# Gate weights of a routed mixture in an fp32 attention and expert kernel: earlier load, products held until landing, one block's logits on one engine

## The chip, the cores and the metric
One Trainium2 chip, one core. The metric is device time in microseconds (us) of one execution. Three runs of the kernel before took 834.63 us in the median (833.44 to 834.67).

## What is computed
Three layers run one after the other, in fp32.

```python
for t in range(S):      # batch 4, 8 heads, S = 768, head_dim 48
    cur = einsum('bhd,bhe->bhde', u * k[t], v[t])
    y[t] = einsum('bhd,bhde->bhe', r[t], state + cur)
    state = w[t][..., None] * state + einsum('bhd,bhe->bhde', k[t], v[t])
h = x @ w_in            # 3072 x 384 -> 2048
x2 = (h * sigmoid(1.702 * h)) @ w_out
logits = x2 @ w_gate    # 8 experts, 384 tokens each
# greedy over all (token, expert) pairs by falling logit, capacity 384
out[mask_e] = relu(x2[mask_e] @ w1[e]) @ w2[e]
```

The order of the logits decides which token goes to which expert, so they are computed to fp32 precision.

## The kernel before
The program is recorded by a planner in Python (class Issue, line 66). Every piece of work is a generator that emits instructions and then yields the engines and times that it expects them to need. The planner keeps a clock and a busy time for each engine and resumes the generators by rank, so its cost figures and its estimates of a load's landing decide the order in which instructions stand on each engine. They do not decide when an instruction runs: on the chip each engine takes its instructions in order and waits on semaphores.

The attention is cut into 24 units of 128 time steps of one batch (unit, line 975), three to a block of 384 tokens. A unit runs decay scans on VectorE (L996, L1001), products of keys and queries with the decays (L1013, L1017, L1020), score matmuls (L1032, L1068), a transpose (L1085), output and state matmuls (L1145, L1150, L1100), and writes its rows of the next layer's input as two halves (L1178 high part, L1181 the subtraction for the low part).

The dense layer (class Ffn, line 1193) runs over 8 blocks and, in each, over 16 slices f of the 2048 columns: nine matmuls of 128x384 into a PSUM buffer g (L1204; high and low parts give three products for each of three row groups), gelu and split (L1250, L1253 on ScalarE, L1256 on VectorE, which frees g), then nine matmuls into three accumulators (L1232), two slices behind. There are two g buffers, so slice f + 2 needs the one of slice f free. Half of block 0 comes first, then block 1, then the rest of block 0, then blocks 2 to 7. The weights come as 16 chunks, each split into high and low parts on VectorE and ScalarE (L773 to L828); for the first nine TensorE corrects each half of a chunk (L806 to L808).

The routing needs logits. For blocks 0 to 6 they are taken from the stored rows of x2 and the gate weights, spread over all 128 partitions (wgB, two tiles, loaded in gate_weights, line 1409): dots (line 1283) multiplies a row tile by two experts' weights at a time on VectorE (L1290) and lets ScalarE sum each of the two (L1279). For block 7 the logits come from TensorE straight from the gelu output (L1464), with w_out times w_gate, formed beforehand in wog and wogp: wog_steps (line 1353) loads the small gate weights wg8, transposes them (L1361), computes four slices on TensorE (L1372, L1384) and the other twelve with dots. The planner puts spin, small bf16 matmuls whose result is not used (L729), into PE's order where its clock has PE waiting.

The places around the change are ORDER (line 691), which sets by hand the first loads on SyncE's (SP) queue; the load and the fixed yield in wog_steps; and the two lines that say when the spread weights count as present:

```python
nc.scalar.dma_start(wg8, dram(w_gate, 0, [[Dm, E], [1, Dm]]))   # L1357
yield 3.0
```

Of the kernel before, what the change touches and what calls it, by code (L numbers as in the profile page):

```python
# [8 lines left out]
F32 = mybir.dt.float32  # L9
# [7 lines left out]
OP = mybir.AluOpType  # L17
# [10 lines left out]
CW = 256  # L28
# [14 lines left out]
def dram(ap, off, dims):  # L43
    return bass.AP(tensor=ap.tensor, offset=ap.offset + off, ap=dims)
# [461 lines left out]
def kernel(ctx, tc, r, k, v, w, rk, u, us, w_in, w_out, w_gate, w1, w2, out):  # L506
    nc = tc.nc
    V, A, P, T = nc.vector, nc.scalar, nc.gpsimd, nc.tensor
    H, D = u.shape
    B, NC = r.shape[:2]  # L510
    Dm = H * D
# [3 lines left out]
    E, NC3 = w1.shape[:2]  # L515
# [3 lines left out]
    KT = Dm // 128  # L519
    cap = NT // E  # L520
    NBLK = NT // NB
# [6 lines left out]
    NCVA, NCVB, NCVC = 3, 2, 3  # L528
# [29 lines left out]
    consts = ctx.enter_context(tc.tile_pool(name="consts", bufs=1))  # L558
    wpool = ctx.enter_context(tc.tile_pool(name="wpool", bufs=32))
    ff = ctx.enter_context(tc.tile_pool(name="ff", bufs=2))  # L560
    cv = ctx.enter_context(tc.tile_pool(name="cv", bufs=1))
# [8 lines left out]
    sc = Issue()  # L570
# [117 lines left out]
    tiny = consts.tile([1, 1], F32, name="tiny")  # L688
    V.memset(tiny, 0.0)
    A.activation(tiny, tiny, AF.Gelu_apprx_sigmoid)  # L690
    ORDER = "0wkr us 1wkr 0v 2wkr W0 1v 2v W1 W2 W3 3wkrv"
    BACK = 6
    back = []
    for x in ORDER.split():
        if x == "us":
            nc.sync.dma_start(usel, us)
        elif x[0] == "W":
            load_w(int(x[1]))
        else:
            load(int(x[0]), x[1:])  # L700
# [571 lines left out]
    router = Router(nc, sc, consts, bank, NJ, E, cap)  # L1272
    WGD = E * Dm // 2
    wgB = []

    def sums(t_, i, put):
        yield from sc.room("A", 0.2)
        for n in range(2):
            A.activation(t_[:, n], t_[:, n], AF.Copy, accum_out=put[n])  # L1279
        yield (("A", 0.85),)  # L1280
        R["cvb"].free(i)

    def dots(x, put, slack, rank):

        for e in range(0, E, 2):
            while not R["cvb"].ok() or sc.busy["V"] > sc.t + slack:
                yield 0.02
            i = R["cvb"].new()
            t_ = cv.tile([128, KT * CW], F32, name="cvb", bufs=NCVB).rearrange("p (a d) -> p a d", a=2)
            V.tensor_tensor(t_, x[:, None, :].to_broadcast([128, 2, Dm]),  # L1290
                            wgB[e // 4][:, (e % 4) * Dm:(e % 4 + 2) * Dm].rearrange("p (a d) -> p a d", a=2), op=OP.mult)
            yield (("V", 0.88),)
            sc.add(sums(t_, i, [put(e + n) for n in range(2)]), rank)

    def logits(j, x2, ring, free_x2):
        while not wgB:
            yield 0.5
        yield from dots(x2, lambda e: router.L[:, j, e:e + 1], 0.5, 2.8)
        free_x2(ring)
        todo[0] -= 1  # L1300

# [22 lines left out]
    def store_x2(blk, tt, acc):  # L1324
        c, b = units[blk * NU + tt]
        j = b * NC + c
        if blk == 0:
            sc.until(lambda: tt in rest)
            x2, ring = rest[tt]
            V.tensor_tensor(x2, acc, x2, op=OP.add)  # L1330
            sc.busy["V"] += 0.55
        else:
            ring = R["cva"].new()
            x2 = cv.tile([128, Dm], F32, name="cva", bufs=NCVA)
            A.activation(x2, acc, AF.Copy)  # L1335
            sc.busy["A"] += 0.49
        stored.add((blk, tt))
        nc.scalar.dma_start(x2d[j * 128:(j + 1) * 128, :], x2)
        if blk < NBLK - 1:
            todo[0] += 1  # L1340
            sc.add(logits(j, x2, ring, R["cva" if blk else "cvc"].free), 4)
        else:
            R["cva"].free(ring)

# [2 lines left out]
    wog = consts.tile([128, NFS, E], F32, name="wog")  # L1347
    wogp = consts.tile([128, NFS * 2 * E + 128], F32R, name="wogp")

    wg8 = consts.tile([E, Dm], F32, name="wg8")  # L1350
    wgT = consts.tile([128, KT, E], F32, name="wgT")

    def wog_steps():

        while ("out", 0) not in wdone:
            yield 0.5
        nc.scalar.dma_start(wg8, dram(w_gate, 0, [[Dm, E], [1, Dm]]))  # L1357
        yield 3.0
        ps, done = yield from bank()
        for kt in range(KT):  # L1360
            T.transpose(ps[:, kt * E:(kt + 1) * E], wg8[:, kt * 128:(kt + 1) * 128], ident[:E, :E])  # L1361
        A.activation(wgT, ps[:, :KT * E].rearrange("p (k e) -> p k e", k=KT), AF.Copy)
        done()
        yield (("T", 0.2), ("A", 0.2))
        for f in range(FPE):
            while ("out", f // 2) not in wdone:
                yield 0.5
            yield from wait("wT")
            ps, done = yield from spare_bank()
            for kt in range(KT):  # L1370
                for n in range(2):
                    T.matmul(ps[:, kt * 128:(kt + 1) * 128], rhs2(f, n)[:, kt * 128:(kt + 1) * 128], identr[0],  # L1372
                             start=(n == 0), stop=(n == 1))
            yield (("T", 0.68),)
            yield from sc.room("A", 0.4)
            i = R["wT"].new()
            wT = s1p.tile([128, KT * 128], F32, name="wT")
            A.activation(wT, ps[:, :KT * 128], AF.Copy)
            done()
            yield (("A", 0.5),)  # L1380
            yield WTLAG
            ps, done = yield from spare_bank()
            for kt in range(KT):
                T.matmul(ps[:, :E], wT[:, kt * 128:(kt + 1) * 128], wgT[:, kt], start=(kt == 0),  # L1384
                         stop=(kt == KT - 1))
            R["wT"].free(i)
            A.activation(wog[:, f], ps[:, :E], AF.Copy)
            done()
            yield (("T", 0.4), ("A", 0.2))
        while len(wgB) < 2:  # L1390
            yield 0.5
        for f in range(FPE, NFS):
            while not R["wT"].ok() or sc.busy["V"] > sc.t + 0.6:
                yield 0.02
            i = R["wT"].new()
            ws = s1p.tile([128, KT * 128], F32, name="wT")
            V.tensor_tensor(ws, rhs2(f, 0).bitcast(F32), rhs2(f, 1).bitcast(F32), op=OP.add)
            yield (("V", 0.48),)
            yield from dots(ws, lambda e: wog[:, f, e:e + 1], 0.6, 2.9)
            R["wT"].free(i)  # L1400
        while R["cvb"].live:
            yield 0.1
        hi, lo = (wogp[:, :NFS * 2 * E].rearrange("p (f x e) -> p f x e", f=NFS, x=2)[:, :, x]
                  for x in range(2))
        A.activation(hi, wog, AF.Copy)
        V.tensor_tensor(lo, wog, hi.bitcast(F32), op=OP.subtract)
        todo[1] = 1

    def gate_weights():
        while ("out", NCH - 1) not in wdone:  # L1410
            yield 1.0
        for i in range(2):
            t_ = cv.tile([128, WGD], F32, name="raw64", bufs=2)
            nc.scalar.dma_start(t_, dram(w_gate, i * WGD, [[0, 128], [1, WGD]]))
            wgB.append(t_)


# [96 lines left out]
    for s in range(len(seq) + 2):  # L1514
# [5 lines left out]
        if s < len(seq):  # L1520
            blk, f = seq[s]
# [264 lines left out]
    for s in range(E * NF3 + 2):  # L1786
        at[0] = s
        i, f = divmod(s, NF3)
# [71 lines left out]
```

## Time and profile before

| | |
|---|---|
| median of 3 runs | 834.63 us (833.44 to 834.67) |
| the profiled execution | 833.22 us, span 831.5 us |
| TensorE matmul busy | 808.4 us, 97% of the span |
| VectorE, ScalarE, GpSimd busy | 622.4, 484.3, 136.3 us |
| granted TensorE clock, mean | 0.991 of full |

The span runs from the first to the last instruction; the execution's time has the start and end around it. PE is TensorE's matmul side, PEld its weight loads, DVE VectorE, ACT ScalarE, POOL GpSimd, SP SyncE; a q behind a name is that engine's queue of DMA issues and semaphores. The first 140 us hold the weights' splitting and the first units, 150 to 500 us the dense layer with the units beside it, 498 to 536 the last block's first products, and the rest the routing and the experts. An instruction's line is that of the kernel's source; for a helper the same line stands for every use.

### The profile page before, as it was taken

What the parts mean: (1) busy time and instruction counts of PE and PEld (TensorE: products, weight loads), DVE (VectorE), ACT (ScalarE), POOL (GpSimd) and SP (SyncE); (2) the same over time, 40 slices, a digit from 0 to 9 for tenths busy, and PEclk for the clock granted to TensorE, in tenths of its full rate; (3) what the DMA queues carried; (4) which work ended last, traced back from release to release, by engine and by line L of the source; (5) the groups of instructions that cost most, each with busy time, mean ns of one, the idle gap of its engine ahead of it and who ended that gap; (6) DMA issues with size and microseconds to landing.
All of it is one profiled execution on the core that took longest, in us unless ns stands there. A gap on an engine that the chain in (4) does not pass through costs nothing.

```text
span 831.5 us, 17525 instructions
## 1 busy us (share of the span) xinstructions
PE 808.4 (97%) x6593; PEld 759.4 (91%) x6593; DVE 622.4 (75%) x1388; ACT 484.3 (58%) x1226; POOL 136.3 (16%) x188
## 2 busy tenths in 40 slices
PE   8999998999999999999999998999999999999996
PEld 7788998899999999999999998988988988999995
DVE  9957797869879969889878827378888987885310
ACT  5653753476676776786597638405466645675421
POOL 1001000000000100000100100003334354454211
PEclk9999998999999999999999999999999999999998
DMA  9823532332322323213302100008989799989400
GB/s 296 234 90 115 173 138 88 90 102 82 94 58 84 93 57 95 82 57 105 105 24 83 36 3 30 1 23 217 209 236 284 218 232 270 280 223 339 89 29 28
DMA packets 46068, 105.85 MB, mean 127 GB/s; under 512 B 7352, under 2 KB 13344, under 8 KB 45984
## 3 DMA queue, kind: packets, MB, share of 16 engines
q1 hardware_dynamic: 30800, 68.20, 25.7%
q0 software_dynamic: 10416, 29.50, 16.3%
q10 hardware_dynamic: 4768, 7.04, 2.3%
q8 instruction: 51, 0.84, 0.4%
q14 instruction: 33, 0.27, 0.1%
HBM read 73.60 MB, written 10.03 MB: 101 GB/s over the span
## 4 chain that ended last, share of the span: by engine, by line
PE 83%; issue 6%; DMA 4%; ACT 3%; DVE 3%; POOL 1%; ACTq 0%; POOLq 0%; DVEq 0%
PE g L1204 31%; PE acc L1232 31%; PE s L1068 3%; PE s L1150 3%; PE s L429 2%; DMA cvb<-x2d,idx 2%; PE s L1145 1%; PE acc L729 1%; PE s L806 1%; PE g L1768 1%; PE s L1085 1%; ACT cvb L1279 1%; PE s L1100 1%; PE s L1685 1%; POOL out L1728 1%
## 5 line engine op out<-in xcount | busy, mean ns | idle before, releaser
L1232 PE MATMUL acc<-wk,gh 128*128 128x384 f32 x1080 | 284.8, 341 | 0.3
L1232 PEld LDWEIGHTS acc<-wk,gh 128*128 128x128 f32 x1080 | 193.7, 189 | 2.1 <-ACT cva L1335 0.5
L1232 PE MATMUL acc<-wk,gl 128*128 128x384 f32 x540 | 182.4, 338 | 0.0
L1204 PE MATMUL g<-xhb,wk 128*128 128x384 f32 x576 | 164.5, 339 | 2.5 <-DVE hold L1256 2.5
L1204 PE MATMUL g<-xha,wk 128*128 128x384 f32 x576 | 166.1, 339 | 0.4 <-DVE gl L1256 0.4
L1279 ACT ACTIVATE cvb<-cvb 128x384 f32<-128x384 f32 x264 | 134.9, 517 | 12.8 <-DVE cvb L1290 10.8
L1250 ACT ACTIVATE g<-g 128x384 f32<-128x384 f32 x128 | 60.8, 475 | 98.9 <-PE g L1204 89.1
L1204 PEld LDWEIGHTS g<-xhb,wk 128*128 128x128 f32 x576 | 105.1, 188 | 3.5 <-DVE hold L1256 3.3
L1204 PEld LDWEIGHTS g<-xha,wk 128*128 128x128 f32 x576 | 105.4, 188 | 1.5 <-DVE gl L1256 0.6
L1232 PEld LDWEIGHTS acc<-wk,gl 128*128 128x128 f32 x540 | 101.8, 188 | 0.1
L1204 PE MATMUL g<-xlb,wk 128*128 128x384 f32 x288 | 97.4, 338 | 0.0
L1204 PE MATMUL g<-xla,wk 128*128 128x384 f32 x288 | 97.1, 337 | 0.0
L1053 POOL TENSOR_SCALAR_AFFINE_SELECT At<-dg 128x512 f32<-128x512 f32 x38 | 30.7, 831 | 377.8 <-DVE dg L1046 280.4
L1256 DVE TENSOR_TENSOR gl<-g,gh 128x384 fp32r<-128x384 f32 x116 | 63.9, 551 | 35.4 <-ACT gh L1253 33.7
L1263 ACT ACTIVATE gh<-g 128x384 fp32r<-128x384 f32 x64 | 31.4, 490 | 88.5 <-PE g L1204 81.2
L1290 DVE TENSOR_TENSOR cvb<-cva,raw 128x768 f32<-128x768 f32 x72 | 68.6, 960 | 16.9 <-ACT cvb L1279 12.3
L1266 DVE SCALAR_TENSOR_TENSOR gl<-g,gh 128x384 fp32r<-128x384 f32 x64 | 35.4, 553 | 41.7 <-ACT gh L1263 41.7
L1253 ACT ACTIVATE gh<-g 128x384 fp32r<-128x384 f32 x116 | 56.7, 489 | 8.8 <-ACT cva L1335 2.3
L1625 ACT ACTIVATE wk<-hold 128x768 fp32r<-128x768 f32 x64 | 52.9, 840 | 9.4 <-DMA hold<-in_w 9.2
L1650 POOL DMA_DIRECT2D wk<-hold x51 | 46.4, 1025 | 64.8 <-ACT wk L1642 38.7
L1204 PEld LDWEIGHTS g<-xla,wk 128*128 128x128 f32 x288 | 54.1, 188 | 0.0
L1204 PEld LDWEIGHTS g<-xlb,wk 128*128 128x128 f32 x288 | 54.1, 188 | 0.0
(280 smaller groups left out, 1259.1 us busy)
## 6 DMA issues: line engine op xcount, KB each, us to landing
hold<-in_w SPq DMA_DIRECT2D x64, 384.0 KB, 7.4
wk<-hold POOLq DMA_DIRECT2D x51, 384.0 KB, 7.7
nat_m<-in_rk SPq DMA_DIRECT2D x15, 384.0 KB, 3.0
nat_v<-in_v SPq DMA_DIRECT2D x22, 256.0 KB, 2.9
raw<-in_w_in SPq DMA_DIRECT2D x7, 768.0 KB, 4.5
raw<-in_w_out SPq DMA_DIRECT2D x7, 768.0 KB, 4.5
nat_w<-in_w SPq DMA_DIRECT2D x22, 226.2 KB, 3.1
nat_k<-in_k SPq DMA_DIRECT2D x22, 224.0 KB, 2.6
```

What stands on the lines that cost most here:

```text
L1053: P.affine_select(At[s], dg[:, s::2][:, :, None].to_broadcast([128, HP, C]), pattern=[[0, HP], [1, C]], compare_op=OP.is_equal, fill=0.0, ...
L1204: T.matmul(p, self.l1(kt, f, a), (self.xh, self.xl)[b_][:, kt], start=(kt == 0 and n == 0), stop=(kt == KT - 1 and n == 2))
L1232: T.matmul(self.acc[tt], gs[a][:, tt * C:(tt + 1) * C], self.r2(f, b_), start=(f in self.cuts and n == 0), stop=(end and n == 2))
L1250: A.activation(p, p, AF.Gelu_apprx_sigmoid)
L1253: A.activation(gh, p, AF.Copy)
L1256: V.tensor_tensor(gl, p, gh.bitcast(F32), op=OP.subtract)
L1263: A.activation(gh, p, AF.Relu)
L1266: V.scalar_tensor_tensor(gl, p, 0.0, gh.bitcast(F32), op0=OP.max, op1=OP.subtract)
L1279: A.activation(t_[:, n], t_[:, n], AF.Copy, accum_out=put[n])
L1290: V.tensor_tensor(t_, x[:, None, :].to_broadcast([128, 2, Dm]), wgB[e // 4][:, (e % 4) * Dm:(e % 4 + 2) * Dm].rearrange("p (a d) -> p a d" ...
L1625: A.activation(Whi[key], raw, AF.Copy)
L1650: P.dma_start(out=Wlo[key].bitcast(F32), in_=raw, accum_op=OP.add)
```

## The change
Three edits.

1. The load of wg8 moves from ACT's queue, in wog_steps, to SP's queue in the initial order, between chunk 1 (W1) and chunk 2 (W2); the 3 us that the planner then let pass are gone.
2. In gate_weights the planner now reckons a landing time for each of the two loads of the spread weights and hands a tile on only when its clock has passed it. The loads follow each other, and no product of dots is recorded before. The planner's cost of a pair of sums on ACT goes from 0.85 to 1.02.
3. The logits of block 6 (NBLK - 2) are made by 24 scalar_tensor_tensor instructions of 128x384 on VectorE, each with its own sum (accum_out), in place of 12 products of 128x768 on VectorE and 24 sums on ScalarE.

```diff
@@ -688,12 +688,15 @@
     tiny = consts.tile([1, 1], F32, name="tiny")
     V.memset(tiny, 0.0)
     A.activation(tiny, tiny, AF.Gelu_apprx_sigmoid)
-    ORDER = "0wkr us 1wkr 0v 2wkr W0 1v 2v W1 W2 W3 3wkrv"
+    ORDER = "0wkr us 1wkr 0v 2wkr W0 1v 2v W1 wg W2 W3 3wkrv"
     BACK = 6
     back = []
+    wg8 = consts.tile([E, Dm], F32, name="wg8")
     for x in ORDER.split():
         if x == "us":
             nc.sync.dma_start(usel, us)
+        elif x == "wg":
+            nc.sync.dma_start(wg8, dram(w_gate, 0, [[Dm, E], [1, Dm]]))
         elif x[0] == "W":
             load_w(int(x[1]))
         else:
@@ -1277,7 +1280,7 @@
         yield from sc.room("A", 0.2)
         for n in range(2):
             A.activation(t_[:, n], t_[:, n], AF.Copy, accum_out=put[n])
-        yield (("A", 0.85),)
+        yield (("A", 1.02),)
         R["cvb"].free(i)
 
     def dots(x, put, slack, rank):
@@ -1292,10 +1295,22 @@
             yield (("V", 0.88),)
             sc.add(sums(t_, i, [put(e + n) for n in range(2)]), rank)
 
-    def logits(j, x2, ring, free_x2):
+    def logits(j, x2, ring, free_x2, late_):
         while not wgB:
             yield 0.5
-        yield from dots(x2, lambda e: router.L[:, j, e:e + 1], 0.5, 2.8)
+        if not late_:
+            yield from dots(x2, lambda e: router.L[:, j, e:e + 1], 0.5, 2.8)
+        else:
+            while not R["cvb"].ok():
+                yield 0.1
+            i = R["cvb"].new()
+            t_ = cv.tile([128, KT * CW], F32, name="cvb", bufs=NCVB)
+            for e in range(E):
+                yield from sc.room("V", 0.4)
+                V.scalar_tensor_tensor(t_[:, :Dm], x2, 1.0, wgB[e // 4][:, (e % 4) * Dm:(e % 4 + 1) * Dm],
+                                       op0=OP.mult, op1=OP.mult, accum_out=router.L[:, j, e:e + 1])
+                yield (("V", 0.6),)
+            R["cvb"].free(i)
         free_x2(ring)
         todo[0] -= 1
 
@@ -1338,7 +1353,7 @@
         nc.scalar.dma_start(x2d[j * 128:(j + 1) * 128, :], x2)
         if blk < NBLK - 1:
             todo[0] += 1
-            sc.add(logits(j, x2, ring, R["cva" if blk else "cvc"].free), 4)
+            sc.add(logits(j, x2, ring, R["cva" if blk else "cvc"].free, blk == NBLK - 2), 4)
         else:
             R["cva"].free(ring)
 
@@ -1347,15 +1362,12 @@
     wog = consts.tile([128, NFS, E], F32, name="wog")
     wogp = consts.tile([128, NFS * 2 * E + 128], F32R, name="wogp")
 
-    wg8 = consts.tile([E, Dm], F32, name="wg8")
     wgT = consts.tile([128, KT, E], F32, name="wgT")
 
     def wog_steps():
 
         while ("out", 0) not in wdone:
             yield 0.5
-        nc.scalar.dma_start(wg8, dram(w_gate, 0, [[Dm, E], [1, Dm]]))
-        yield 3.0
         ps, done = yield from bank()
         for kt in range(KT):
             T.transpose(ps[:, kt * E:(kt + 1) * E], wg8[:, kt * 128:(kt + 1) * 128], ident[:E, :E])
@@ -1412,6 +1424,9 @@
         for i in range(2):
             t_ = cv.tile([128, WGD], F32, name="raw64", bufs=2)
             nc.scalar.dma_start(t_, dram(w_gate, i * WGD, [[0, 128], [1, WGD]]))
+            ready = sc.dma(2.3)
+            while sc.t < ready:
+                yield 0.2
             wgB.append(t_)
```

The planner rebuilds the order of everything between about 34 us and the end of the dense layer. Lines after the edits move by 3 to 12 (L1256 becomes L1259, L1290 becomes L1293). The numbers of each instruction stay as they were but for block 6's logits, the one load, and spin: 28 of its matmuls stand in PE's order ahead of block 1's first product where 10 stood, and three single ones in the last block are gone.

On PE, the transposes of wg8 (s<-ident,wg) stood behind the first twelve L1232 of block 0 and ahead of the correction of chunk 3:

```order
L1232 MATMUL acc_623<-wk,gl 128x384
L1232 MATMUL acc_621<-wk,gh 128x384 x2
L1232 MATMUL acc_621<-wk,gl 128x384
L1361 MATMUL s_654<-ident,wg_167 128x8 x3
L806 MATMUL s_659<-cvc,ident 128x384
L807 MATMUL s_659<-wk,identr_146 128x384
L808 MATMUL s_659<-wk,identr_145 128x384
L1372 MATMUL s_671<-identr_145,wk 128x128 x6
```

Now, still on PE, they stand between the two halves of chunk 2's correction:

```order
L809 MATMUL s_614<-cvc,ident 128x384
L810 MATMUL s_614<-wk,identr_148 128x384
L811 MATMUL s_614<-wk,identr_147 128x384
L1373 MATMUL s_621<-ident,wg_107 128x8 x3
L809 MATMUL s_627<-cvc,ident 128x384
L810 MATMUL s_627<-wk,identr_148 128x384
L811 MATMUL s_627<-wk,identr_147 128x384
L1384 MATMUL s_636<-identr_147,wk 128x128 x6
L1235 MATMUL acc_649<-wk,gh 128x384 x2
```

So the transposes moved ahead of twelve L1232 and of half a chunk.

On DVE, in unit 6 (the first of block 2, behind the last chunk), the first product with the spread weights (cvb<-wT,raw) stood inside the unit's chain:

```order
L1001 SCALAR_TENSOR_TENSOR Fw<-nat_w_78,lead_139 112x516
L1397 TENSOR_TENSOR wT<-wk 128x384
L1013 TENSOR_TENSOR At_1647<-nat_r_80,nat_k_82 112x512
L1256 TENSOR_TENSOR gl<-g_1617,gh 128x384
L1290 TENSOR_TENSOR cvb<-wT,raw_1632 128x768
L1017 TENSOR_TENSOR nat_k_82<-nat_k_82,Q 112x512
L1020 TENSOR_TENSOR nat_r_80<-nat_r_80,Fw 112x512
```

Now, on DVE at the same unit:

```order
L1004 SCALAR_TENSOR_TENSOR Fw<-nat_w_78,lead_141 112x516
L1259 TENSOR_TENSOR gl<-g_1611,gh 128x384
L1016 TENSOR_TENSOR At_1640<-nat_r_80,nat_k_82 112x512
L1020 TENSOR_TENSOR nat_k_82<-nat_k_82,Q 112x512
L1023 TENSOR_TENSOR nat_r_80<-nat_r_80,Fw 112x512
L1027 TENSOR_TENSOR S_155<-S_155,Q 112x4x48
L1076 COPY_PREDICATED At_1640<-later,s_1668 128x512
```

The unit's chain goes through without the product, and the first one (L1293) comes only after unit 7's chain.

On DVE, in the last block, the logits of block 6 (cvb<-cva,raw) stood between the subtractions that free the g buffers (gl for f = 1, hold from f = 2 on):

```order
L1290 TENSOR_TENSOR cvb<-cva,raw_1632 128x768 x2
L1256 TENSOR_TENSOR gl<-g_5803,gh 128x384
L1290 TENSOR_TENSOR cvb<-cva,raw_1632 128x768
L1290 TENSOR_TENSOR cvb<-cva,raw_1634 128x768
L1256 TENSOR_TENSOR hold<-g_5840,hold 128x384
L1290 TENSOR_TENSOR cvb<-cva,raw_1634 128x768
L1290 TENSOR_TENSOR cvb<-cva,raw_1632 128x768
L1256 TENSOR_TENSOR hold<-g_5884,hold 128x384
```

Now, on DVE up to the subtraction for f = 4:

```order
L1310 SCALAR_TENSOR_TENSOR cvb,L<-cva,raw_1627 128x384 x4
L1259 TENSOR_TENSOR gl<-g_5821,gh 128x384
L1310 SCALAR_TENSOR_TENSOR cvb,L<-cva,raw_1627 128x384 x3
L1259 TENSOR_TENSOR hold<-g_5859,hold 128x384
L1310 SCALAR_TENSOR_TENSOR cvb,L<-cva,raw_1694 128x384
L1310 SCALAR_TENSOR_TENSOR cvb,L<-cva,raw_1627 128x384
L1310 SCALAR_TENSOR_TENSOR cvb,L<-cva,raw_1694 128x384 x3
L1259 TENSOR_TENSOR hold<-g_5900,hold 128x384
L1310 SCALAR_TENSOR_TENSOR cvb,L<-cva,raw_1694 128x384 x2
L1310 SCALAR_TENSOR_TENSOR cvb,L<-cva,raw_1627 128x384
L1310 SCALAR_TENSOR_TENSOR cvb,L<-cva,raw_1694 128x384
L1310 SCALAR_TENSOR_TENSOR cvb,L<-cva,raw_1627 128x384
L1259 TENSOR_TENSOR hold<-g_5930,hold 128x384
```

Ahead of the subtraction for f = 4 (the last row) stand 17 of the new instructions and three subtractions; from there on it is two new ones to a subtraction, and then one.

## Rows read from the trace of the kernel before

**Rows 1.** The page, busy time, share of the span, instructions of each engine.
```profile
PE 808.4 (97%) x6593; PEld 759.4 (91%) x6593; DVE 622.4 (75%) x1388; ACT 484.3 (58%) x1226; POOL 136.3 (16%) x188
```

**Rows 2.** Three stretches: busy time of each engine (instructions), clock, DMA share, GB/s.
```profile
41.00:46.00 5.00, 5.00 (x21) 4.33 (x20) 4.87 (x7) 2.54 (x5) 0.00 (x0) 0.66 0.64 216
140.00:148.00 8.00, 6.23 (x54) 5.24 (x56) 5.96 (x10) 2.80 (x10) 0.57 (x1) 0.57 0.19 62
200.00:500.00 300.00, 300.00 (x2350) 286.79 (x2349) 243.08 (x387) 203.27 (x638) 25.77 (x36) 1.00 0.24 71
```

**Rows 3.** Waits of PE: line, waited for: us in total, times, longest.
```profile
PE s L1068 <- DVE nat_r L1020: 2.7, 1, 2.7
PE g L1204 <- DVE hold L1256: 2.5, 3, 1.5
```

**Rows 4.** Timeline, first place: start, us, engine, instruction [idle before].
```profile
28.88 0.98 ACT L773 ACTIVATE cvc<-wk 128x384 f32<-128x384 f32 x2
...
34.18 0.59 ACTq L1357 DMA_DIRECT2D wg<-in_w_gate  x1
...
40.04 0.35 PE L1361 MATMUL s<-ident,wg 8*128 8x8 f32 x3 [1.64 <-DMA wg<-in_w_gate]
...
88.79 0.73 PE L729 MATMUL acc<-ident 128*128 128x128 bf16 x10
```

**Rows 5.** Timeline, second place and the unit after it.
```profile
130.19 0.95 DVE L821 TENSOR_TENSOR cvc<-cvc,cvb 128x768 f32<-128x768 f32 x1
...
134.43 0.82 ACTq L1414 DMA_DIRECT2D raw<-in_w_gate  x2
...
135.49 0.69 DVE L1013 TENSOR_TENSOR At<-nat_r,nat_k 112x512 f32<-112x512 f32 x1
...
137.34 0.95 PE L1032 MATMUL s<-usel,At 112*128 112x2 f32 x8
...
139.10 0.98 DVE L1290 TENSOR_TENSOR cvb<-wT,raw 128x768 f32<-128x768 f32 x1 [2.45 <-DMA raw<-in_w_gate]
...
141.77 2.08 PE L1068 MATMUL s<-nat_r,nat_k 48*128 48x128 f32 x16 [2.67 <-DVE nat_r L1020]
...
148.75 0.44 PE L1232 MATMUL acc<-wk,gl 128*128 128x384 f32 x1
...
154.93 0.95 PE L1032 MATMUL s<-usel,At 112*128 112x2 f32 x8
...
161.56 0.62 PE L1232 MATMUL acc<-wk,gh 128*128 128x384 f32 x2
```

**Rows 6.** Timeline, last block: block 6's logits on DVE, slices f = 4 and on.
```profile
498.80 1.85 DVE L1290 TENSOR_TENSOR cvb<-cva,raw 128x768 f32<-128x768 f32 x2 [2.58 <-ACT cva L1335]
...
506.07 0.33 PE L1204 MATMUL g<-xhb,wk 128*128 128x384 f32 x1
...
510.24 0.23 PE L729 MATMUL acc<-ident 128*128 128x128 bf16 x1
...
512.01 0.44 PE L1204 MATMUL g<-xhb,wk 128*128 128x384 f32 x1 [1.54 <-DVE hold L1256]
```

**Rows 7.** The chain that ended last, undisturbed steps of the last block.
```profile
525.41 1.56 PE g L1204 x9
526.98 0.36 PE s L1464 x2
```

**Rows 8.** Single lines: duration ns min/median/max, first and last start us, forms.
```profile
L781 DVE SCALAR_TENSOR_TENSOR cvc<-raw,cvc x14: 957/959/959, 20.9 to 126.1; 128x768 int32<-128x768 int32 x14
L781 DVE SCALAR_TENSOR_TENSOR cvc<-wk,cvc x4: 551/554/559, 30.5 to 34.6; 128x384 int32<-128x384 int32 x4
...
L1279 ACT ACTIVATE cvb<-cvb x264: 504/516/545, 140.1 to 522.1; 128x384 f32<-128x384 f32 x132
L1279 ACT ACTIVATION_READ_ACCUMULATOR cvb<-cvb x264: 182/192/223, 140.5 to 522.5; 128x1 f32 x132
...
L1290 DVE TENSOR_TENSOR cvb<-wT,raw x48: 926/952/981, 139.1 to 443.5; 128x768 f32<-128x768 f32 x48
...
L1256 DVE TENSOR_TENSOR gl<-g,gh x116: 527/551/560, 31.5 to 533.8; 128x384 fp32r<-128x384 f32 x116
```

## The prediction

> **What bounds the kernel now.** I began with the page: TensorE (PE) is busy 808.4 of 831.5 us, VectorE (DVE) 622.4, ScalarE (ACT) 484.3 [rows 1]. A busy PE may still be a slow PE, so the stretches came next: from 200 to 500 us PE is busy 300.00 of 300 us at granted clock 1.00 [rows 2], and there only fewer products could help. In two other stretches the mean clock is 0.66 and 0.57. The granted clock has two levels, 1.2 and 2.4 GHz, so 0.66 over 5 us is 3.4 us at half clock, and that costs 1.7 us of work. Third, the list of PE's waits shows what it stood still for: 2.7 us for L1020 and 2.5 us in three waits for L1256 [rows 3], 1.64 us for the DMA of the small gate weights [rows 4]. Those are the three places the change touches, and the slow stretches follow the first and the last of these waits.
>
> **Place 1, the small gate weights (34 to 46 us).** The load is issued on ACT's queue at 34.18; its transposes stand in PE's order at 40.04, after a wait of 1.64 us for it, and the half clock comes right behind [rows 4, 2]. The change puts the load on SP's queue ahead of the third chunk's two halves. Its issue took 0.59 us on ACT, so what follows on SP is at most so much later. The first reader of those halves is ACT at 28.88, which shows no idle time ahead of it [rows 4]; I cost the move at nothing, and were that cover gone, at 0.6 us. In the new PE order the transposes stand right behind the first half of chunk 2's correction, near 35.2 us on the old clock. The load took 5.8 us when it was issued at 34.18, and it now leaves some 25 us ahead of its reader.
>
> So 1.64 + 1.7 = 3.3 us go. Against that, the new order has 18 more of spin's small matmuls ahead of block 1's first product (28 for 10). The 10 take 0.73 us [rows 4], 18 take 1.3 us, and I charge them in full, the dear end. Place 1 gives **2.0 us**; between 0 (the rebuilt order makes PE wait elsewhere before 90 us) and 3.3 (the spins fall into a wait).
>
> **Place 2, the spread gate weights (134 to 149 us).** Two 768 KB loads are issued at 134.43, and DVE sits 2.45 us before the first product that reads them, at 139.10. Queued behind that product on DVE are L1017 and L1020, and PE's L1068 waits for L1020 until 141.77 [rows 5], then runs at half clock to about 147.5 [rows 2]. To price it I take the next unit, which had neither: from its L1032 to the end of its L1100 are 154.93 to 161.56, 6.63 us, with 11 dense products between; here 137.34 to 148.75, 11.41 us, with 8 [rows 5]. One dense product is 1.56 / 9 = 0.173 us [rows 7]. So 11.41 - (6.63 - 3 x 0.173) = **5.3 us** are lost there.
>
> In the new DVE order no product with the spread weights stands before the unit's chain; the first comes after the whole next unit, some 16 rows later. What is late next? L1013 of the unit, which PE's L1032 waits for. In the old run DVE goes from L821 at 130.19 to the end of L1013 at 136.18 [rows 5]; the new order has one subtraction (0.55, [rows 8]) in the place of L1397, an instruction of the same shape, so 136.2 again if DVE were not earlier at all. PE, 2.0 us earlier and with L1032 two products sooner, stands there at 137.34 - 2.0 - 0.35 = 135.0: a wait of 1.2 us. But the new order finishes chunk 8 (DVE's L790) ahead of block 1's third subtraction instead of behind it, five DVE steps of 0.55 to 0.96 us each [rows 8] earlier, and from there to L821 DVE works through the chunks almost without a gap. I therefore take no wait; the other end is 1.2 us of wait plus 1.7 us of slow clock as in place 1, so 2.4 to 5.3 us.
>
> Holding the products back moves the products that read them, of 0.95 us each, about 10 us later. Those on w_out ended at 443.5 [rows 8]; their result is first read in the last block, a few us before the 506.07 of [rows 6]. The landing estimate and the 1.02 in place of 0.85 are only the planner's; they change the order, not a duration.
>
> **Place 3, logits of the last block but one (498 to 523 us).** Before: 12 DVE products of 0.96 us, each waiting for two ACT sums of 0.52 us [rows 8]; ACT is full, the g buffers come free late, and PE stands 2.5 us in three waits plus three lone spins of 0.23 us: 3.2 us [rows 3, 6]. After: 24 DVE instructions of 128x384 with a sum, no ACT. ACT loses 24 x 0.52 = 12 us and is no longer in the chain. DVE starts at 498.80 [rows 6], and before it can free the g buffer of f = 4 it has 17 new instructions and four subtractions of 0.56 us (the dear end of [rows 8]) in its order: with c for one instruction it ends at 498.80 + 17c + 2.24. PE wants that buffer for f = 6, two steps of 1.92 us [rows 7] after 506.07 [rows 6], at 509.91, with about 0.1 us of signalling. PE's new wait is 17c - 8.76, nothing below c = 0.515. Later groups are two instructions and one subtraction, 2c + 0.56 against 1.92, and add nothing below c = 0.68.
>
> c is not in the trace. Scalar-tensor-tensor of this shape from two SBUF sources takes 0.554 [rows 8], the lower end. ACT's sum carries a second instruction, a read of 0.19, that overlaps the next one almost wholly [rows 8]; a DVE read of that size with no overlap gives 0.75. I take 0.62, a third of the way, since ACT's pair is the nearest row. New wait 1.8, gain 3.2 - 1.8 = **1.4 us**; ends: +2.5 at 0.554, and -1.1 at 0.75 (3.9 us, and 0.4 in the later groups).
>
> The Trainium skill ("VectorE: DVE Perf Modes", section Two Vector instructions with no wait between them) says that an instruction which also writes its accumulator out is two instructions, main and read. The trace shows this on ACT only [rows 8]; with the read fully paid the sum would be 828.4, the second rival below.
>
> **Sum.** 2.0 + 5.3 + 1.4 = 8.7 us off the profiled execution's 833.22: 824.5. The median of the runs, 834.63, lies 1.4 above that execution, so the forecast is **825.9 us**. What follows 523 us keeps its order and moves up as a whole.
>
> **Rivals.**
> - *DVE is not early at place 2.* For it: DVE is the fuller of the other engines. Against: chunk 8's place in the order. 1.2 to 2.9 us less: 827.1 to 828.8. Chance 0.15.
> - *The accumulator's read costs its full 0.19.* For it: it is an instruction of its own on ACT. Against: there it hides. Place 3 turns from +1.4 to -1.1: 828.4. Chance 0.15.
> - *The new instruction runs at half rate.* Its second 384 elements' worth is 0.959 - 0.554 = 0.405 by the rows of 768 and 384 elements [rows 8], so c = 0.96, the new wait is 7.6, later groups add 3 x 0.56 = 1.7, and place 3 is 9.3 - 3.2 = 6.1 us worse than before: 833.4, no change that shows. For it: two four-byte SBUF sources and a sum at once, a form the trace lacks. Against: without the sum, the same sources run at the same rate as any product. Chance 0.05. By the Trainium skill ("Vector Engine (DVE) Microarchitecture Reference", section Points that are easy to get wrong) such an instruction with two non-bf16 SBUF sources does run at half throughput; the rows without a sum [rows 8] speak against it.
> - *Slower: DVE becomes the bound of the last block and the clock falls with it.* If c reaches about 0.95, PE waits about 4 us for the buffer of f = 3 (12c - 7.4 by the same sum) and 3.5 us for that of f = 4, longer than the 2.7 us [rows 3] after which it ran slow at place 2. Two such slow stretches of 1.7 to 2.6 us on top of 833.4: 837 to 839. It decides from c = 0.95 up. Chance 0.05.
> - *No change.* The rebuilt order, which differs on every engine from 34 to 500 us, gives the gain back in waits that the old order did not have. Against: PE has none in 200 to 500. 834.6. Chance 0.05.
>
> **How the numbers follow.** My forecast has 0.55. The range 823.0 to 831.5 takes in all best ends (3.3 + 5.3 + 2.5 = 11.1: 823.5, less the runs' scatter) and place 2 and 3 at their worst together (825.9 + 2.9 + 2.5 = 831.3); it leaves out the last three cases, 0.15. A measurement of this kernel can tell about 0.2%, 1.7 us, from no change: faster 0.85, same 0.10, slower 0.05.
>
> **What would show it.** In the profile after: no PE wait for the small weights, the transposes near 35.5, clock 1.00 from 41 to 46 and through the first unit of block 2; no DVE wait for the spread weights; in the last block but one's logits 24 new DVE instructions near 0.6 us, with PE's longest wait, near 1.8 us, at f = 6. A clock below 1.00 after either of the first two places, or new instructions of 0.75 us or more, would prove the sum wrong.

## The result and the profile after

| | before | after |
|---|---|---|
| median | 834.51 us (833.44 to 834.67, 4 runs) | 821.40 us (821.03 to 822.38, 4 runs) |
| ratio, 95% interval | | 0.9847 (0.983 to 0.9864) |
| profiled execution | 833.22 us, span 831.5 | 822.38 us, span 820.4 |
| granted clock, mean | 0.991 | 0.998 |
| end of the dense layer (start of the last nine products) | 533.98 | 521.73 |

The change takes 13.1 us off the median; by the ratio it is 1.53%. The forecast was 825.9 with a range from 823.0 on. The sign was right, and the three places gained; the size was not right: 8.7 us were forecast, two thirds of what came.

The page, busy time of each engine:

```profile
PE 803.3 (98%) x6608; PEld 756.6 (92%) x6608; DVE 622.8 (76%) x1424; ACT 472.7 (58%) x1178; POOL 140.6 (17%) x188
```

Against [rows 1], ACT is 11.6 us lighter, about the 24 sums of 0.52 us, and DVE is where it was. PE is busy 5.1 us less for the same products and 15 more spins. That is clock won back: the half clock of [rows 2] took 0.34 x 5 + 0.43 x 8 = 5.1 us.

The three places in time, and the steady stretch (columns as in [rows 2]):

```profile
41.00:46.00 5.00, 5.00 (x31) 4.33 (x30) 3.53 (x6) 2.84 (x7) 0.00 (x0) 1.00 0.81 262
130.00:140.00 10.00, 10.00 (x107) 9.01 (x106) 8.27 (x15) 2.96 (x8) 1.23 (x2) 1.00 0.66 216
140.00:148.00 8.00, 8.00 (x97) 7.15 (x96) 5.91 (x11) 2.90 (x9) 1.22 (x2) 1.00 0.41 121
200.00:500.00 300.00, 300.00 (x2303) 287.61 (x2303) 245.34 (x411) 203.97 (x639) 28.20 (x34) 1.00 0.24 70
500.00:525.00 25.00, 24.89 (x151) 24.54 (x150) 10.90 (x30) 11.51 (x24) 1.60 (x3) 1.00 0.00 1
```

The two slow stretches of [rows 2], at 0.66 and 0.57, now stand at 1.00 with PE busy all through. 200 to 500 us is as full as it was, so nothing was gained there.

PE's waits from 20 to 540 us, all that the list shows:

```profile
PE s L809 <- DVE At L1076: 0.3, 1, 0.3
PE s L1071 <- DVE nat_r L1023: 0.2, 1, 0.2
```

Of [rows 3] the 2.5 us for L1256 (now L1259) are gone altogether, and so are the 2.7 us of L1071 (old L1068): the 0.2 us that the list has for it stand at 158.2, in a later unit. The 1.64 us of [rows 4] for the small weights are gone too. Their transposes now run at 35.23, where 35.2 to 35.5 was expected:

```profile
35.23 0.35 PE L1373 MATMUL s<-ident,wg 8*128 8x8 f32 x3
```

In the first unit of block 2 the chain goes through on DVE (L1016 to L1023), and PE's L1035 and L1071 (old L1032, L1068) show no wait. The first product with the spread weights, the last row, comes only behind the next unit's chain, without a wait on DVE:

```profile
130.01 0.68 DVE L1016 TENSOR_TENSOR At<-nat_r,nat_k 112x512 f32<-112x512 f32 x1
...
130.76 1.04 PE L1035 MATMUL s<-usel,At 112*128 112x2 f32 x8
131.34 0.68 DVE L1023 TENSOR_TENSOR nat_r<-nat_r,Fw 112x512 f32<-112x512 f32 x1
...
132.54 1.16 PE L1071 MATMUL s<-nat_r,nat_k 48*128 48x128 f32 x16
...
144.86 0.93 DVE L1293 TENSOR_TENSOR cvb<-wT,raw 128x768 f32<-128x768 f32 x1
```

The new instruction, first as single lines (duration ns min/median/max), then in DVE's timeline:

```profile
L1310 DVE SCALAR_TENSOR_TENSOR cvb<-cva,raw x24: 545/551/558, 490.4 to 506.7; 128x384 f32<-128x384 f32 x24
L1310 DVE DVE_READ_ACCUMULATOR cvb<-cva,raw x24: 78/81/83, 490.8 to 507.1; 128x1 f32 x24
```

```profile
490.36 0.56 DVE L1310 SCALAR_TENSOR_TENSOR cvb<-cva,raw 128x384 f32<-128x384 f32 x1 [2.58 <-ACT cva L1350]
...
494.60 0.55 DVE L1259 TENSOR_TENSOR hold<-g,hold 128x384 fp32r<-128x384 f32 x1
495.07 0.55 DVE L1310 SCALAR_TENSOR_TENSOR cvb<-cva,raw 128x384 f32<-128x384 f32 x1
495.54 0.08 DVE L1310 DVE_READ_ACCUMULATOR cvb<-cva,raw 128x1 f32 x1
495.54 0.55 DVE L1310 SCALAR_TENSOR_TENSOR cvb<-cva,raw 128x384 f32<-128x384 f32 x1
496.02 0.08 DVE L1310 DVE_READ_ACCUMULATOR cvb<-cva,raw 128x1 f32 x1
496.02 0.55 DVE L1310 SCALAR_TENSOR_TENSOR cvb<-cva,raw 128x384 f32<-128x384 f32 x1
...
500.42 0.56 DVE L1259 TENSOR_TENSOR hold<-g,hold 128x384 fp32r<-128x384 f32 x1
```

These rows hold the main error of the prediction. An instruction lasts 0.55 us, but the next one starts 0.47 to 0.48 us after it (495.07, 495.54, 496.02): two neighbours overlap by about 0.08. The accumulator's read is there, lasts 0.08 and starts together with the next instruction. It costs nothing that shows: the subtraction at 494.60, of the same shape and without such a read, is followed after 0.47 us too. c, as the formula uses it, is 0.478 us, the mean over the five instructions from 495.07 to the next subtraction at 497.46; I had 0.62. The last row is the subtraction for f = 4. It ends at 500.98, and PE starts f = 6 at 501.46 without a wait.

The end of the dense layer, by its last nine products in the chain that ended last, before and after:

```profile
533.98 1.56 PE acc L1232 x9
```

```profile
521.73 1.56 PE acc L1235 x9
```

From here the gain can be split. DVE's first logit of block 6 starts at 490.36 where it started at 498.80 [rows 6]: 8.4 us come from places 1 and 2, for which 2.0 + 5.3 = 7.3 were forecast. The end of the dense layer is 12.25 us earlier: 3.8 us come from place 3, for which 1.4 were forecast. The 8.4 can be split where PE has done the same matmuls in both orders, spins not counted. It starts the 671st at 92.87 before and 89.69 after, and the 1133rd, just behind the first units of block 2, at 161.56 and 153.35; at the 101st the two were level. So place 1 gave 3.2 us and place 2 5.0, which is 8.2 of the 8.4. Behind the dense layer this profile is 1.2 us longer than the one before (298.7 for 297.5 us to the end of the span), in a part that the change does not touch.

### The profile page after: what moved, and what is told of

Its sections match the earlier page's. It is cut to its first block, busy times and chain, and to the rows that moved or that the text cites. A ratio compares the mean times of both kernels' runs of the same rounds, so it can differ in the third digit from the quotient of the medians.

```text
span 820.4 us, 17510 instructions
## 1 busy us (share of the span) xinstructions
PE 803.3 (98%) x6608; PEld 756.6 (92%) x6608; DVE 622.8 (76%) x1424; ACT 472.7 (58%) x1178; POOL 140.6 (17%) x188
## 4 chain that ended last, share of the span: by engine, by line
PE 84%; issue 6%; DMA 5%; DVE 2%; POOL 1%; ACT 1%; SPq 0%; POOLq 0%; ACTq 0%; DVEq 0%
PE g L1207 33%; PE acc L1235 33%; PE s L1071 3%; PE s L1153 3%; PE s L429 2%; DMA cvb<-x2d,idx 2%; PE s L809 2%; PE s L1148 1%; DMA hold<-in_w 1%; DMA nat_v<-in_v 1%; PE s L1088 1%; PE s L1103 1%; PE acc L732 1%; PE s L1479 1%; POOL out L1743 1%
## 5 line engine op out<-in xcount | busy, mean ns | idle before, releaser
L1282 ACT ACTIVATE cvb<-cvb 128x384 f32<-128x384 f32 x240 | 122.7, 517 | 8.4 <-DVE cvb L1293 7.9
L1056 POOL TENSOR_SCALAR_AFFINE_SELECT At<-dg 128x512 f32<-128x512 f32 x38 | 35.0, 944 | 361.1 <-DVE dg L1049 273.5
L1259 DVE TENSOR_TENSOR gl<-g,gh 128x384 fp32r<-128x384 f32 x116 | 63.5, 548 | 29.1 <-ACT gh L1256 28.9
L1266 ACT ACTIVATE gh<-g 128x384 fp32r<-128x384 f32 x64 | 31.4, 491 | 88.8 <-PE g L1207 81.5
L1293 DVE TENSOR_TENSOR cvb<-cva,raw 128x768 f32<-128x768 f32 x60 | 57.2, 963 | 8.5 <-ACT cva L1350 4.8
L1256 ACT ACTIVATE gh<-g 128x384 fp32r<-128x384 f32 x116 | 56.5, 487 | 6.5 <-ACT cva L1350 2.4
```

The costliest lines, as they stand in the source:

```text
L1056: P.affine_select(At[s], dg[:, s::2][:, :, None].to_broadcast([128, HP, C]), pattern=[[0, HP], [1, C]], compare_op=OP.is_equal, fill=0.0, ...
L1256: A.activation(gh, p, AF.Copy)
L1259: V.tensor_tensor(gl, p, gh.bitcast(F32), op=OP.subtract)
L1266: A.activation(gh, p, AF.Relu)
```

## Experiments

**One edit at a time.** Three kernels, each the kernel before with one edit, ran beside 26 executions of the kernel before (median 832.46).

Edit 1 alone:

```diff
-    ORDER = "0wkr us 1wkr 0v 2wkr W0 1v 2v W1 W2 W3 3wkrv"
+    ORDER = "0wkr us 1wkr 0v 2wkr W0 1v 2v W1 wg W2 W3 3wkrv"
...
-        nc.scalar.dma_start(wg8, dram(w_gate, 0, [[Dm, E], [1, Dm]]))
-        yield 3.0
```

> The kernel before with edit 1 alone (small gate weights on SP's queue between chunks 1 and 2, the planner's 3 us gone). Theory (three places add up): the wait of 1.64 us and the 1.7 us of half clock behind it go, 18 more spins cost about 1.3 us, places 2 and 3 stay as they were: 2.0 us off 834.5, 832.5, between 831.0 (spins free) and 834.5. Rival (the rebuilt order gives the gain back before 100 us, and place 2 makes the whole result): 834.5, within 0.5. The trace is to show the granted clock 1.00 from 41 to 46 us, 0.66 before.

Measured: ratio 0.9959 (0.9946 to 0.9971), 3.4 us of 834.5, with an interval of 2.4 to 4.5. That is near the best end of the place's range (3.3), not the 2.0 of its sum, although the 18 spins stand in this kernel too. The clock from 41 to 46 us is 1.00, and PE starts its 671st matmul at 89.91, 3.0 us earlier than before. The earlier load and the 3 us of the planner were not tried apart.

Edit 2's wait for the landing alone (the cost stays 0.85):

```diff
             nc.scalar.dma_start(t_, dram(w_gate, i * WGD, [[0, 128], [1, WGD]]))
+            ready = sc.dma(2.3)
+            while sc.t < ready:
+                yield 0.2
             wgB.append(t_)
```

> The kernel before with the landing wait of the two spread gate weights in the planner alone (ACT's cost stays 0.85). Theory: DVE's 2.45 us wait, PE's 2.67 us wait and the half clock to 147.5 us go: 5.3 to 6 us off 834.5, 828.5 to 829.2. Rival (DVE is not early and L1013 is late next): 2.4 to 4.1 us off, 830.4 to 832.1, with a PE wait of about 1.2 us before L1032. Second rival (place 2 gave more than it lost at its own wait, because the whole order behind it is better): 7 us or more off, under 827.5.

Measured: ratio 0.9949 (0.993 to 0.9967), 4.3 us, with an interval of 2.8 to 5.8 that holds the forecast 5.3. The rival of a late DVE asked for a PE wait of 1.2 us before L1032; there is none. Its time, 2.4 to 4.1 us off, lies inside the interval as well, so it falls by the trace and not by the time. The second rival, 7 us or more, lies outside the interval. In the profile PE starts the 671st matmul 1.6 us earlier than before, with the clock at 1.00 at place 1, where PE's order is the old one, and the 1133rd 6.6 us earlier: 5.1 us for place 2.

Edit 3 alone, with the new branch of logits as the change has it:

```diff
-            sc.add(logits(j, x2, ring, R["cva" if blk else "cvc"].free), 4)
+            sc.add(logits(j, x2, ring, R["cva" if blk else "cvc"].free, blk == NBLK - 2), 4)
```

> The kernel before with edit 3 alone (block 6's logits as 24 instructions with their own sum on VectorE). Theory (the instruction's start-to-start time is 0.478 us, so the wait 17c - 8.76 is nothing): all of the 2.5 us of PE waits and 0.7 us of lone spins go, 3.2 to 3.9 us off 834.5, 830.6 to 831.3. Rival (my c of 0.62 holds when the code stands alone): 1.4 us off, 833.1. Second rival (the gain in the whole change came from the cost of 1.02, which frees ACT before the last block): no gain here, 834.5.

Measured: ratio 0.9945 (0.9922 to 0.9969), 4.6 us. My c of 0.62 would have given 1.4, outside the interval of 2.6 to 6.5. In the profile the first logit starts at 496.78 and the last nine products at 528.15, so place 3 alone gives (533.98 - 498.80) - (528.15 - 496.78) = 3.8 us, as in the whole change. PE's stretch from 500 to 525 us, with no wait left:

```profile
500.00:525.00 25.00, 25.00 (x145) 1.00 0.02 7
```

The three parts add: 0.41 + 0.51 + 0.55 = 1.47%, and the whole gave 1.53%.

**The price of c.** In two kernels the new instruction is issued more often, so that c grows: each one twice, and every second one twice.

All doubled:

```diff
-                V.scalar_tensor_tensor(t_[:, :Dm], x2, 1.0, wgB[e // 4][:, (e % 4) * Dm:(e % 4 + 1) * Dm],
-                                       op0=OP.mult, op1=OP.mult, accum_out=router.L[:, j, e:e + 1])
+                for _ in range(2):
+                    V.scalar_tensor_tensor(t_[:, :Dm], x2, 1.0, wgB[e // 4][:, (e % 4) * Dm:(e % 4 + 1) * Dm],
+                                           op0=OP.mult, op1=OP.mult, accum_out=router.L[:, j, e:e + 1])
```

Half of them doubled, the same with

```diff
+                for _ in range(1 + e % 2):
```

> The whole change with each of the 24 new instructions issued twice (the second writes the same sum again), the planner's cost unchanged: c is then 0.956 us in place of 0.478. Theory (the buffers' formula): DVE frees f = 1 at 495.1, f = 3 at 503.7 and f = 4 at 508.9 us of this profile's clock, so PE waits 1.0, 3.2 and 3.3 us and three times about 0.5: 9.0 us over 821.4, 830.4 at full clock. If the granted clock also falls behind the two waits of over 3 us, as it did behind the 2.67 us at place 2, 1.7 to 2.9 us each are added: 834 to 836. Rival (ACT or another engine set the end in the last block, and DVE has room): under 2 us, 821.4 to 823.4.

> The whole change with every second one of the 24 new instructions issued twice: the mean c is 0.717 us, near the dear end of the prediction. Theory (the buffers' formula, from this change's own times): DVE frees f = 3 at 500.8 and f = 4 at 504.9 us, PE wants them at 499.55 and 501.46, so it waits 1.3 and 2.1 us, 3.4 to 3.5 us in all, nothing after f = 6; by the prediction's own 17c - 8.76 it is 3.4. Without a fall of the clock 3.5 us over the whole change, a ratio of 0.989 to 0.991. Rival (the clock falls behind the 2.1 us wait as it did at place 2): 1.7 to 2.9 us more, 0.991 to 0.994.

Measured: ratio 1.0011 (0.9997 to 1.0025) with all doubled, and 0.9921 (0.9898 to 0.9945) with half. PE's waits in the last block, all doubled:

```profile
497.43 0.44 PE L1207 MATMUL g<-xhb,wk 128*128 128x384 f32 x1 [0.98 <-DVE gl L1259]
507.00 0.61 PE L1207 MATMUL g<-xhb,wk 128*128 128x384 f32 x1 [3.65 <-DVE hold L1259]
512.86 0.44 PE L1207 MATMUL g<-xhb,wk 128*128 128x384 f32 x1 [2.13 <-DVE hold L1259]
520.98 0.45 PE L1207 MATMUL g<-xhb,wk 128*128 128x384 f32 x1 [0.52 <-DVE hold L1259]
```

and with half of them doubled:

```profile
494.33 0.44 PE L1207 MATMUL g<-xhb,wk 128*128 128x384 f32 x1 [0.19 <-DVE gl L1259]
500.89 0.44 PE L1207 MATMUL g<-xhb,wk 128*128 128x384 f32 x1 [0.90 <-DVE hold L1259]
505.55 0.45 PE L1207 MATMUL g<-xhb,wk 128*128 128x384 f32 x1 [2.46 <-DVE hold L1259]
```

The prediction's formula against the sum of these waits:

| c, us | 17c - 8.76 | PE's waits, measured |
|---|---|---|
| 0.478 | -0.6 | none |
| 0.717 | 3.4 | 3.55 |
| 0.956 | 7.5 | 7.28 |

The formula is within 0.2 us of these sums; the number put into it was wrong. With all doubled the clock fell too, as the slower rival had it. This is PE from 506 to 520 us:

```profile
506.00:520.00 14.00, 10.88 (x43) 0.76 0.00 1
```

0.24 of 14 us is 3.4 us beside the waits. With half of them doubled the clock from 500 to 525 us stayed at 1.00.

The formula leaves two things out. For the later groups the prediction adds 1.7 us at a c of 0.96, which makes 9.2 with all doubled; of the 7.28 only 0.52 stand behind f = 6, and a PE at half clock also wants its buffers later. And a wait costs more here than the time that PE stands. Nine products take 1.56 us undisturbed [rows 7]; behind the longest wait with half doubled they took

```profile
505.55 1.84 PE g L1207 x9
```

From the first logit to the last nine products it is 31.4 us in the change, 36.3 with half doubled and 43.1 with all: 4.9 and 11.7 us more, where waits and clock make 3.55 and 10.7. So half doubled, at 0.9921, lies above the 0.989 to 0.991 that I expected, though its interval reaches into it. It lies where the rival with the falling clock had put it, but the clock did not fall; the 1.4 us beyond the waits were not traced further than the row above.

**What was too slow before: VectorE's products or ScalarE's sums?** DVE's part weighs the same in both kernels: 12 products of 0.93 to 0.96 us, some 0.90 from start to start (two take 1.85 in [rows 6]), against 24 x 0.478 = 11.5. So I put the old products back and left out the sums, that is, block 6's logits are not computed and two elements of each product stand in for them:

```diff
-            for e in range(E):
+            for e in range(0, E, 2):
                 yield from sc.room("V", 0.4)
-                V.scalar_tensor_tensor(t_[:, :Dm], x2, 1.0, wgB[e // 4][:, (e % 4) * Dm:(e % 4 + 1) * Dm],
-                                       op0=OP.mult, op1=OP.mult, accum_out=router.L[:, j, e:e + 1])
-                yield (("V", 0.6),)
+                V.tensor_tensor(t_.rearrange("p (a d) -> p a d", a=2), x2[:, None, :].to_broadcast([128, 2, Dm]),
+                                wgB[e // 4][:, (e % 4) * Dm:(e % 4 + 2) * Dm].rearrange("p (a d) -> p a d", a=2), op=OP.mult)
+                V.tensor_copy(router.L[:, j, e:e + 2], t_[:, 0:2 * Dm:Dm])
+                yield (("V", 1.2),)
```

> The whole change with block 6's logits as the old 12 products of 128x768 on VectorE, the sums on ScalarE left out (two elements of each product stand in for the two sums, copied by VectorE, so the logits of block 6 are not computed). Theory (before, DVE's products were not too long, they waited for ACT's sums; DVE's load is the same, 12 x 0.93 + 12 copies of about 0.1 = 12.4 us for 24 x 0.478 = 11.5): the time of the whole change within 1 us, and no PE wait over 0.7 us from 480 to 515 us. Rival (the new instruction gains because it is quicker on DVE than the products): 1.5 to 3.9 us over the whole change, with the old waits for the subtraction back.

Measured: ratio 0.9859 (0.9831 to 0.9888), no different from the whole change. The interval alone would leave room for the lower part of the rival's range; the trace does not. From the first logit to the last nine products it is 31.9 us, for 31.4 in the change and 35.2 before, and PE waits for the subtraction once, for 0.3 us:

```profile
PE g L1207 <- DVE hold L1259: 0.3, 1, 0.3
```

So the products were not too long. They stood behind ACT: each pair had to wait for two sums of 0.52 us before its buffer came free, and ACT had its gelu and splits between. In the kernel before, DVE waited 5.2 us for ACT's sums between 495 and 525 us, and its subtraction, which frees the g buffers, 4.3 us for ACT's split:

```profile
DVE cvb L1290 <- ACT cvb L1279: 5.2, 7, 1.6
DVE hold L1256 <- ACT hold L1253: 4.3, 3, 1.9
```

**The whole change again, and three variants,** run together (before: 836.23).

> The whole change once more, beside the next three. Theory (three places add up): the parts alone gave 0.41, 0.51 and 0.55 per cent; their sum, 1.47 per cent, makes a ratio of 0.9853, and the mean granted clock stands at 0.997 or 0.998 in every execution. Rival (the parts help each other, or the first measurement was lucky): under 0.983 or over 0.988.

Measured: 824.03 us, ratio 0.9866 (0.9832 to 0.9899). The sum of the parts, 0.9853, lies inside. The clock was 0.996, 0.997, 0.996 and 0.992, not always as high as expected.

Without the 28 spins ahead of block 1's first product:

```diff
-            if self.spin and n % 1 == 0:
+            if self.spin and (self.t < 60 or not self.strict):
```

> The whole change without the 28 spins ahead of block 1's first product (10 of them the kernel before had too); no work of the result is left out. Theory (the spins stand where PE would wait, since edit 1 alone gave 3.4 us, all of wait and clock): the time of the whole change within 0.6 us, with PE waits of 1 to 2 us between 60 and 90 us in their place. Rival (they cost what I charged, 1.3 us for 18, 2.1 us for 28): 1.3 to 2.1 us under the whole change. Second rival (PE's wait there lowers the clock): 1 to 2 us over it.

Measured: 824.17 us, ratio 0.9858 (0.9824 to 0.9892), the same as the whole change. These are PE's waits from 50 to 140 us without the spins; the whole change has only the third row there.

```profile
PE g L1207 <- DVE gl L1259: 0.5, 1, 0.5
PE g L1207 <- DVE xla L1184: 0.4, 1, 0.4
PE s L809 <- DVE At L1076: 0.3, 1, 0.3
PE g L1207 <- ACT xha L1181: 0.2, 1, 0.2
```

1.1 us of waits take the place of the spins. The medians, with intervals of 5.7 us, could not tell 1.3 us, but the traces can: PE starts the 651st matmul at 83.70 us in the whole change again and at 83.68 without the spins, and the 801st at 112.09 and 112.29. The spins stand where PE would lose the time anyway, so the 1.3 us that I charged for 18 of them was a cost only on paper.

The planner's cost of a pair of sums back at 0.85:

```diff
-        yield (("A", 1.02),)
+        yield (("A", 0.85),)
```

> The whole change with the planner's cost of a pair of sums back at 0.85. Theory (the cost moves the order where PE has no wait): the time of the whole change within 0.8 us. Rival (ACT's truer cost keeps it ahead before the last block and is part of the gain there): 1 to 3 us over the whole change, with PE waits for L1259 from 480 us on.

Measured: 823.84 us, ratio 0.9853 (0.9823 to 0.9884). This part of edit 2 does nothing that can be measured.

The logits of all blocks 0 to 6 in the new form:

```diff
-            sc.add(logits(j, x2, ring, R["cva" if blk else "cvc"].free, blk == NBLK - 2), 4)
+            sc.add(logits(j, x2, ring, R["cva" if blk else "cvc"].free, True), 4)
...
-                yield (("V", 0.6),)
+                yield (("V", 0.48),)
```

> The whole change with the logits of all of blocks 0 to 6 in the new form, the planner's cost of one at 0.48. Theory (VectorE pays 24 x 0.478 = 11.5 us a block for 12 x 0.95 = 11.4, ScalarE loses 12.5 us a block, and PE waits for neither between 200 and 490 us): the time of the whole change within 0.8 us, plus up to 1.6 us for 22 more spins that the planner puts before the last block. Rival (ScalarE's time sets the buffers' release in the units): 1 to 3 us under the whole change.

Measured: 828.53 us, ratio 0.9916 (0.9889 to 0.9943), 4.5 us over the whole change on the same chip, so that both theories miss. The rebuilt order has a wait that none of the others had, and a slower clock behind it:

```profile
PE s L1071 <- ACT gh L1256: 0.9, 1, 0.9
```

```profile
158.00:163.00 5.00, 4.63 (x42) 0.66 0.75 238
```

0.9 us of wait, 0.34 x 5 = 1.7 us of clock and 22 spins of 1.40 us together before the last block make 4.0. The dense layer ends 4.3 us later than in the whole change on the same chip (525.91 against 521.59). Relieving ScalarE where PE does not wait for it brought nothing, and the new order cost something. Why the planner's order came out worse just there stays open. None of the variants beats the change.

## Why the prediction was wrong in size and right in kind

- *What bounds the kernel.* Right. The gain lies in the two slow stretches and the three groups of waits, and none of it between 200 and 500 us.
- *Place 1, "I charge them in full, the dear end": 2.0 us.* Too low. The wait and the half clock went as forecast. The 18 spins cost nothing that shows, by the run without spins; the profile gained 3.2 us here, and edit 1 alone gave 3.4. The range's end of 3.3, spins that fall into a wait, was the truth. I could have read it before: the planner puts a spin only where its own clock has PE waiting.
- *Place 2: 5.3 us.* Right in mechanism and in size: 5.0 us in the profile, 5.1 in that of edit 2 alone, whose time gave 4.3 with an interval that holds all three. DVE was early, as argued from chunk 8's place: its L1016 ended at 130.69, 5.5 us before the old 136.18. But PE did not come to L1032 at 135.0, as the sum had it. It came at 130.76, since 20 dense products fewer stand ahead of it (367 for 387) and not two. That DVE was still 0.07 us ahead is luck as far as this sum goes.
- *Place 3, "Scalar-tensor-tensor of this shape from two SBUF sources takes 0.554, the lower end ... I take 0.62": 1.4 us.* This step failed: c measured 0.478, and the place gave 3.8 us. The duration of one instruction is not what it costs its engine in a row of them, so even the lower end was too high. The trace of before had the right number in a row that I did not use:

```profile
34.12 1.03 DVE L781 SCALAR_TENSOR_TENSOR cvc<-wk,cvc 128x384 int32<-128x384 int32 x2
```

  Two instructions of 0.554 us take 1.03 together, so the second starts 1.03 - 0.55 = 0.48 after the first. With c = 0.48 the formula gives 17 x 0.48 - 8.76 = -0.6, no wait, and place 3 gives all 3.2 us; 3.8 came, since PE had lost more than the time it stood, as with half doubled. The sum would have been 2.0 + 5.3 + 3.2 = 10.5, or 11.8 with free spins.
- *The accumulator's read paid in full (0.15).* Wrong. It is an instruction of 0.08 us and starts together with the next one. The Trainium skill ("VectorE: DVE Perf Modes", section Two Vector instructions with no wait between them) calls such an operation two instructions; the trace agrees, and shows no start delayed by the second.
- *Half rate (0.05).* Wrong: 0.478 us from start to start, not 0.96. The Trainium skill ("Vector Engine (DVE) Microarchitecture Reference", section Points that are easy to get wrong) says that a form with two non-bf16 SBUF sources halves its throughput. Here both sources are f32 in SBUF with a sum besides, and the measurement decides against it.
- *Slower from c = 0.95 (0.05).* Did not happen at c = 0.478. The doubled kernel shows that the mechanism is real: 7.28 us of waits, a clock of 0.76 and a ratio of 1.0011, about 835.4, where the rival had 837 to 839.
- *The range.* Its best end added 2.5 us for place 3, the gain at c = 0.554. A duration taken for a lower bound closed the range on the side where the result came. Place 3 at its 3.8 us would still have put the forecast at 823.5, inside the range; the 1.2 us of place 1 and the step to the median, below, took the result out of it.

The sum as a whole: without the step to the median the forecast was 824.5, and the profiled execution after took 822.38. Of these 2.1 us, place 3 made 2.4 and places 1 and 2 together 1.1; the part behind the dense layer took 1.2 back, and the time outside the span 0.3. The other 2.4 us between forecast and median are the 1.4 that I added for the step from profile to median, and the 1.0 by which the profiled execution after lies above its own median. That step took for granted that the profiled execution lies under its median in both kernels. It did not, and on which side it falls is chance.

## What to carry to other kernels

Price a run of instructions on one engine by the distance from start to start, which the timeline gives wherever a row groups two or more, and never take the duration of one as the lower end. When an engine seems too slow for its buffers, see whether it works or waits for the engine behind it: here VectorE's load stayed the same, and taking ScalarE out of the handshake removed every wait. Fillers that a planner puts in where it sees idle time should be priced at nothing first, as 28 of them came out here.

## What was not expected of the hardware

The clock's slow spells are not tied to one wait in every execution. With the landing wait alone, PE stood 1.5 us for the small weights as before, and the clock stayed at 1.00 where the profile of before had 0.66. With all new instructions doubled, it stood at 0.88 from 46 to 60 us with PE busy all the time and no wait ahead. These are the two stretches (PE busy, clock, DMA share, GB/s):

```profile
41.00:46.00 5.00, 5.00 (x29) 1.00 0.51 162
```

```profile
46.00:60.00 14.00, 14.00 (x91) 0.88 0.17 59
```

In 41 executions of the kernel before, beside the experiments, the mean clock lay between 0.987 and 0.995; the eight of the whole change had 0.992 to 0.998. So a loss of clock read from one profile, such as the 1.7 us of place 1, holds for that execution. An estimate of the average, from each execution's span and mean clock: 6.5 us are lost in the 41 of before and 2.9 in the eight of the whole change, so some 3.6 us of the gain are clock, where the two profiles alone have 5.1 up to the last block.
